# Two more LN2 tiles of the first block transposed by DMA, two more FFN blocks in halves, tile 3 loaded ahead of the keys' weight, and a new instruction order

## The chip, the cores and the metric

The kernel runs on one core of one Trainium2 chip. The metric is the device time of one launch in microseconds (us); a kernel's time is the median of several runs. Five engines work at once, each in the order of its own instruction list: TensorE (PE, matrix products and transposes), VectorE (DVE), ScalarE (ACT), GpSimd (POOL) and SyncE (SP), which here issues all the DMAs. They wait for each other through semaphores only where data or a buffer demands it.

## The reference

A linear-attention block and a feed-forward block, both with a layer norm ahead of them and a residual around them, on 2048 tokens of width 512, with 32 heads of 16 and a hidden width of 1792, in bf16:

```python
phi = lambda t: jnp.where(t > 0, t + 1, jnp.exp(t)) + 1e-6
pq, pk = phi(q), phi(k)
kv  = jnp.einsum("bhsd,bhse->bhde", pk, v)
z   = jnp.einsum("bhsd->bhd", pk)
num = jnp.einsum("bhqd,bhde->bhqe", pq, kv)
den = jnp.einsum("bhqd,bhd->bhq", pq, z)[..., None] + 1e-6
...
h  = x + _A_ref(_layernorm(x, axis=-1), A_wqkv, A_wo)   # q, k, v = layernorm(x) @ wqkv; (num / den) @ wo
h2 = h + _B_ref(_layernorm(h, axis=-1), B_w1, B_w2)     # relu(layernorm(h) @ w1) @ w2
```

## The kernel before

The order of all work is written out by hand in the string `ORDER`: 564 words, each of which emits one small group of instructions. `lx.3.1` loads one token tile from tile 3 on, `K.0.4` makes the keys of tile 0 in PSUM bank 4, and so on. The words are emitted in sequence, and each engine gets its own in that sequence; a word's place matters against the other words of its engine, and for waits against what it reads. Nothing is scheduled by a compiler.

The 2048 tokens are 16 tiles of 128 (`NT`), and 4 chunks of 512 (`NCH`), tiles 4c to 4c+3 being chunk c. PSUM has 8 banks of 128x512 f32; the bank is written into the words of PE (last number or second number), so a product waits until the bank's last contents have been read.

**Loads and first layer norm.** SP issues the loads of x (`lx`, line 214), then those of the weights (`lk` keys, `lq` queries, later `lv`, `lo`, `l1`, `l2`, line 220). For each tile t: `S.t`, `A.t` (DVE, mean and variance, lines 248, 249), `R.t.n` (ACT, two small instructions for the reciprocal deviation, lines 254, 255), `N.t` (DVE, line 262). The result must be transposed into `lnT[c]`: tiles 0 to 4 by PE (`T.t.bank`, four 128x128 transposes, line 287) with a copy by ACT (`E.t`, line 297), tiles 5 to 15 by a DMA transpose issued by SP (`X.t`, line 308). The words `warm` ahead of all this are products on zeros with no reader.

**Keys, queries, statistics.** `K.t` (line 316) and `Q.c.j` (line 324) are four products of 512 columns each. phi is made as `F`/`qF` (ACT, exp), `U`/`qU` (ACT, relu), `M`/`qM` (DVE), `D`/`qD` (DVE, line 344). `G.t` (line 368) adds tile t's layer norm times pk into banks 4 to 7, over all 16 tiles. The column sum z is gathered from DVE sums of tiles 2 to 9 (`za`, `zf`, `zhi`, `zlo`) and from the other tiles by forty products of one column (`z`, line 392), whose last operands are pk of tiles 14 and 15, written by `D.14.2`. Then come `zc`, `zh` on DVE, and `gA`/`gD`, `kv`, `kx`, `m`, `mA`/`mD`, which make the folded matrix `m_sb`.

**Denominators.** For chunk c: `d4` (PE, line 440; one word may do two chunks), `dl4` and `dx4` (ACT, lines 446, 451), `wb.c` (SP writes the reciprocals to DRAM, line 468), eight words `rb.c.h` (SP reads them back broadcast over heads into `rr`, line 471), `dm.c` (DVE, two instructions, line 484: queries times `rr` into `pqs`). `rr` is one buffer for all four chunks.

**Attention output and second layer norm.** `h.t` (PE, four products, line 493), `hD.t` (DVE, adds x), `s.t`, `a.t` (DVE, statistics), `r` (ACT, reciprocal deviations of four tiles), `n.t` (DVE, line 270) or `nA.t` (ACT, line 276) for the centred, negated tile in `hn`. It is transposed into `lnT[c]` either by SP with a DMA transpose (`x.t`, line 309) or by PE with a DVE copy (`t.t.bank`, line 287, and `v.t`, line 306). In the first chunk tiles 0 and 1 go by DMA, 2 and 3 by PE. All later tiles go by DMA.

**FFN.** `p.c.f` (PE, line 508) makes block f of 14 of the hidden layer for the 512 tokens of chunk c, four products of 512 columns. `ph.c.f.bank.half` (line 517) does the same for 256 tokens, four products of 256 columns, so that half 0 needs only tiles 0 and 1 of the chunk. Chunk 0 has blocks 0 to 3 in halves and the other ten whole. `pD` (DVE) or `pA` (ACT) empties two banks into `acts`. `f.t` (PE, line 537), `fo.t` (DVE, line 545) and `fd.t` (SP) make and store the output of tile t; the columns of the last tile are done in three parts.

Of the kernel before, what the change touches and what calls it, by code (L numbers as in the profile page):

```python
# [57 lines left out]
def kernel(  # L58
# [166 lines left out]
    def op_tw(n):
        rows = A_wqkv.rearrange("(r s) n -> r s n", s=A_wqkv.shape[0] // n)
        nc.scalar.dma_start(out=first_w[0:n, 0, :], in_=rows[:, 0, D : D + 4])

    def op_tx(n):
        rows = xf.rearrange("(r s) d -> r s d", s=S // n)  # L230
        nc.scalar.dma_start(out=first_x[0:n, :], in_=rows[:, 0, 0:4])

    def op_ta():
        nc.scalar.dma_start(out=first_w[:], in_=wqkv_v[:, :, D : D + 4])
# [234 lines left out]

    def op_rb(c, h):  # L470
        nc.sync.dma_start(
            out=rr[h * DH : (h + 1) * DH, :, :],
            in_=scr[c][:, h, :, :].rearrange("j o n -> o j n").broadcast_to([DH, KD, CW]),
        )
# [6 lines left out]

    def op_dm(c, jb, n):
        i = (c * KD + jb) % NQ
        nc.vector.tensor_tensor(  # L484
            out=pqs[:, i : i + n, :], in0=pqT[c][:, jb : jb + n, :], in1=rr[:, jb : jb + n, :], op=ALU.mult
        )


# [99 lines left out]
```

## Time and profile before

| what | value |
|---|---|
| median of three runs (lowest, highest) | 169.46 us (169.15, 169.84) |
| the profiled execution: its time | 169.66 us |
| the profiled execution: its span, first to last instruction | 168.0 us |
| granted TensorE clock, mean | 1.00 |
| DVE busy, ACT busy | 115.6 us, 49.5 us |

The span is what the trace shows; the profiled execution's time is 1.66 us longer than its span, for what lies around it. All durations come from this one execution. In the trace a product's own duration includes the filling and draining of its pipeline; products that follow each other overlap, so what a product costs PE is read from the chain of waits or from the distance of start times. "Idle before" is the time an engine stood still ahead of an instruction, with what ended it. In the rows, `x4` counts the instructions that a row merges.

### The profile page before, as it was taken

How to read it: one execution, taken by the hardware profiler on the slowest of the kernel's cores; microseconds unless marked ns; L12 is line 12 of the kernel's file. 1: busy time of each engine (PE TensorE's matmuls, PEld its weight loads, DVE VectorE, ACT ScalarE, POOL GpSimd, SP SyncE). 2: the span in 40 equal slices, each digit the busy share in tenths (PEclk: the TensorE clock that was granted, in tenths of full speed). 3: DMA queues.
4: the chain of work that ended last, by engine and by line, in shares of the span. 5: the costliest groups of instructions: out<-in, count | busy, mean ns of one | idle time of the engine just before them, and what ended most of it. 6: DMA issues, size and time to landing. Idle time of an engine off the chain costs nothing.

```text
span 168.0 us, 2417 instructions
## 1 busy us (share of the span) xinstructions
PE 162.7 (97%) x924; PEld 79.2 (47%) x924; DVE 115.6 (69%) x217; ACT 49.5 (29%) x83; POOL 4.8 (3%) x21
## 2 busy tenths in 40 slices
PE   7799999999999999999999999999999999999992
PEld 7444444454544754444444444444444447444442
DVE  3899999942579999999999755764144773432312
ACT  3799968715798843100101000000000000000000
POOL 7400000000000000000000000000000000000000
PEclk9999999999999999999999999999999999999999
DMA  4984054681595364414552520000101000011021
GB/s 108 353 298 88 20 106 95 189 301 45 132 337 161 98 205 132 132 48 123 83 102 57 126 63 0 0 0 0 62 31 35 0 0 7 32 34 48 31 94 39
DMA packets 25003, 16.01 MB, mean 95 GB/s; under 512 B 15008, under 2 KB 23968, under 8 KB 24992
## 3 DMA queue, kind: packets, MB, share of 16 engines
...
q8 instruction: 7, 0.11, 0.3%
...
## 4 chain that ended last, share of the span: by engine, by line
PE 92%; DMA 4%; SPq 2%; DVE 1%; issue 0%
PE bk L537 28%; PE bk L508 27%; PE bk L324 8%; PE bk L368 8%; PE bk L493 8%; PE bk L316 7%; DMA wq_sb<-in_A_wqkv_dram 4%; PE bk L517 2%; SPq L214 2%; PE bk L440 1%; DVE gT L545 1%; PE bk L392 1%; PE bk L414 1%; PE bk L426 1%; PE bk L287 0%
## 5 line engine op out<-in xcount | busy, mean ns | idle before, releaser
L537 PE MATMUL bk<-w_sb,at 128*128 128x512 bf16 (+2 forms) x252 | 50.0, 355 | 0.0
L508 PE MATMUL bk<-lnT,w_sb 128*128 128x512 bf16 x208 | 46.9, 379 | 0.0
L528 DVE TENSOR_SCALAR at<-bk 128x1024 bf16<-128x1024 f32 x27 | 32.8, 1223 | 13.2 <-PE bk L508 13.2
L537 PEld LDWEIGHTS <-at 128*128 128x128 bf16 x252 | 23.5, 98 | 25.4
L508 PEld LDWEIGHTS <-w_sb 128*128 128x128 bf16 x208 | 20.4, 98 | 23.9
L545 DVE SCALAR_TENSOR_TENSOR gT<-bk,rstd,h_nat 128x512 bf16<-128x512 f32 (+2 forms) x18 | 12.4, 691 | 24.6 <-PE bk L537 22.0
L334 ACT ACTIVATE eb<-bk 128x1024 bf16<-128x1024 f32 (+1 forms) x18 | 16.6, 929 | 5.3 <-PE bk L316 2.8
L337 ACT ACTIVATE rb<-bk 128x1024 bf16<-128x1024 f32 (+1 forms) x18 | 16.4, 929 | 0.0
L324 PE MATMUL bk<-lnT,wq_sb 128*128 128x512 bf16 x64 | 15.1, 379 | 0.3 <-DMA wq_sb<-in_A_wqkv_dram 0.3
L316 PE MATMUL bk<-wk_sb,lnT 128*128 128x512 bf16 x64 | 15.3, 379 | 0.0
L493 PE MATMUL bk<-m_sb,pqs 128*128 128x512 bf16 x64 | 15.1, 379 | 0.0
L368 PE MATMUL bk<-at,h_nat 128*128 128x512 bf16 x56 | 13.1, 379 | 0.0
L248 DVE BATCH_NORM_STATS2 st<-x_nat 128x6 f32<-128x512 bf16 x16 | 10.6, 678 | 2.3 <-DMA x_nat<-in_A_x_dram 2.3
L499 DVE TENSOR_TENSOR h_nat<-bk,x_nat 128x512 bf16<-128x512 f32 x16 | 10.6, 676 | 0.9 <-PE bk L493 0.9
L254 ACT ACTIVATE rstd<-mv,eps 128x2 f32<-128x2 f32 (+2 forms) x14 | 4.2, 297 | 23.7 <-DVE mv L251 20.9
L250 DVE BATCH_NORM_STATS2 st<-h_nat 128x6 f32<-128x512 bf16 x16 | 10.5, 684 | 0.1
L324 PEld LDWEIGHTS <-wq_sb 128*128 128x128 bf16 x64 | 6.1, 98 | 7.7 <-DMA wq_sb<-in_A_wqkv_dram 0.8
L493 PEld LDWEIGHTS <-pqs 128*128 128x128 bf16 x64 | 6.1, 98 | 7.7 <-DVE pqs L484 0.6
L368 PEld LDWEIGHTS <-h_nat 128*128 128x128 bf16 x64 | 6.1, 98 | 7.3 <-issue 0.2
L316 PEld LDWEIGHTS <-lnT 128*128 128x128 bf16 x64 | 6.1, 98 | 6.8
L341 DVE TENSOR_SCALAR eb<-eb 128x1024 bf16<-128x1024 bf16 (+1 forms) x18 | 6.6, 389 | 0.0
L262 DVE TENSOR_SCALAR h_nat<-x_nat,mv,rstd 128x512 bf16<-128x512 bf16 x16 | 6.3, 408 | 0.2 <-ACT rstd L255 0.2
...
## 6 DMA issues: line engine op xcount, KB each, us to landing
...
x_nat<-in_A_x_dram SPq DMA_DIRECT2D x2, 512.0 KB, 7.9
...
wk_sb<-in_A_wqkv_dram SPq DMA_DIRECT2D x1, 512.0 KB, 4.1
...
wq_sb<-in_A_wqkv_dram SPq DMA_DIRECT2D x1, 512.0 KB, 6.2
```

The costliest lines, as they stand in the source:

```text
L248: op_S = lambda t: nc.vector.bn_stats(out=st[:, t, :], in_=x_nat[:, t, :])
L316: nc.tensor.matmul(bk[:, b, :], lhsT=lnT[c][:, kd, j * P : (j + 1) * P], rhs=wk_sb[:, kd, :], start=(kd == 0), stop=(kd == KD - 1),)
L324: nc.tensor.matmul(bk[:, b, :], lhsT=wq_sb[:, kd, j * P : (j + 1) * P], rhs=lnT[c][:, kd, :], start=(kd == 0), stop=(kd == KD - 1),)
L334: nc.scalar.activation(out=buf(eb, kind, i, n), in_=bank(at_bank[kind, i], n), func=ACT.Exp)
L337: nc.scalar.activation(out=buf(rb, kind, i, n), in_=bank(at_bank[kind, i], n), func=ACT.Relu)
L368: nc.tensor.matmul(bk[:, KD + kd, :], lhsT=ln_nat[:, t, kd * P : (kd + 1) * P], rhs=pk(t)[:, 0, :], start=(not stated), stop=(len(stated) ...
L493: nc.tensor.matmul(bk[:, b, :], lhsT=pqs[:, (c * KD + jb) % NQ, j * P : (j + 1) * P], rhs=m_sb[:, jb, :], start=(jb == 0), stop=(jb == KD ...
L499: nc.vector.tensor_tensor(out=h_nat[:, t : t + n, :], in0=bank(at_bank["h", t], n), in1=x_nat[:, t : t + n, :], op=ALU.add,)
L508: nc.tensor.matmul(bk[:, b, :], lhsT=w1_sb[:, kd, f * P : (f + 1) * P], rhs=lnT[c][:, kd, :], start=(kd == 0), stop=(kd == KD - 1),)
L528: nc.vector.tensor_scalar(out=acts[c % 2][:, f : f + n, :], in0=bank(at_bank["p", c, f], n), scalar1=-1.0, scalar2=0.0, op0=ALU.mult, op1= ...
L537: nc.tensor.matmul(bk[:, b, 0 : w * P], lhsT=acts[c % 2][:, f, j * P : (j + 1) * P], rhs=w2_sb[:, f, k * P : (k + w) * P], start=(f == 0), ...
L545: nc.vector.scalar_tensor_tensor(out=o_t[:, t % NO, cols], in0=bk[:, at_bank["f", t, k], 0 : w * P], scalar=rstd2[:, t : t + 1], in1=h_nat ...
```

## The change

1. `lx.3.1` (load of tile 3) is issued before `lk.0.4` (the keys' weight) instead of after it.
2. `t.2`, `t.3` and their DVE copies `v.2`, `v.3` are gone; `x.2`, `x.3` (DMA transposes on SP) take their place. SP's list there becomes `wb.1 x.3 x.1 x.0 x.2 rb.1...` instead of `wb.1 x.1 x.0 rb.1...`. ACT makes the centred tile 3 (`nA.3`), DVE those of tiles 0, 1, 2; before, ACT made 0 and 1 and DVE 2 and 3.
3. FFN blocks 6 and 7 of chunk 0 are made in halves too: `ph` occurs 12 times instead of 8, `p` 50 times instead of 52.
4. `rr` becomes two buffers, used by chunk parity (`rr[c % 2]`). Four helpers that no word calls, and the two tiles they wrote, are deleted.
5. The whole `ORDER` is new. On PE, all four `T` of the first tiles stand ahead of `K.1`, and half of `K.3` ahead of the first `Q`; between `K.12` and `z` there are other `G`s, with eleven tiles' `G` ahead of `z` in place of twelve; `h.3`, `h.1` follow two of chunk 2's `Q`s in place of four; the first eight words after `Q.3` are halves.

PE's list around the loads, the sums and the second layer norm, before and after:

```
before: T.0 T.1 K.0 T.2 K.1 T.3 K.2 Q.0.3 T.4 Q.0.1 K.3 Q.0.0 K.4 ...
after:  T.0 T.1 K.0 T.2 T.3 K.1 K.2 K.3(first half) Q.0.0 K.3(second half) T.4 Q.0.1 Q.0.3 K.4 ...

before: ... K.12 G.7 K.11 K.10 G.8 K.14 K.15 G.9 G.6 G.10 G.11 z G.14 d4.0 G.13 G.12 G.15 Q.1.1 ...
after:  ... K.12 G.5 K.11 K.10 K.14 K.15 G.8 G.4 G.9 G.6 G.7 G.10 z G.14 d4.0 G.15 G.11 G.12 G.13 Q.1.1 ...

before: Q.2.0 Q.2.1 Q.2.3 Q.2.2 h.1 d4.1 h.0 h.2 h.3 Q.3.0 Q.3.1 Q.3.3 Q.3.2 t.2 t.3
        ph.3.0 ph.1.0 ph.2.0 ph.3.1 ph.0.0 ph.0.1 ph.2.1 p.7 d4.2 ph.1.1 p.6 h.4 ...
after:  Q.2.1 Q.2.0 h.3 h.1 d4.1 h.0 Q.2.2 Q.2.3 h.2 Q.3.2 Q.3.3 Q.3.0 Q.3.1
        ph.2.0 ph.3.0 ph.6.0 ph.7.0 ph.6.1 ph.7.1 ph.1.0 d4.2 ph.3.1 ph.2.1 ph.0.1 ph.0.0 ph.1.1 p.4 p.5 h.7 ...
        (ph.f.half, chunk 0)
```

The diff, with the two strings cut to the places that the prediction speaks of:

```diff
-table const masks warm.70.7.64 warm.2.7 lx.0.1 S.0 A.0 R.0.1 lx.1.1 S.1 lx.2.1 A.1 N.0 T.0.1 lk.0.4 S.2 R.1.1
-N.1 T.1.2 lx.3.1 A.2 E.0 K.0.4 R.2.1 lx.4.2 S.3 N.2 T.2.1 E.1 A.3 S.5 R.3.1 K.1.0.0.2 K.1.0.2.2 N.3 S.4 A.5 A.4
-E.2 T.3.2 K.2.6.0.2 K.2.6.2.2 F.0.1 M.0.1 lx.6.2 E.3 S.7 lq.0.4 R.4.2 lx.8.4 Q.0.3.1 N.4 U.0.1 A.7 F.1.1 F.2.1
...
-qD.1.2.2 mA.2.2 qF.2.0.2 Q.2.2.0 qU.2.0.2 dm.0.2.2 dm.0.0.2 qM.2.0.2 h.1.6 hD.1 s.1 a.1 qU.2.2.2 d4.1.3 dl4.1
-h.0.7 hD.0 s.0 dx4.1 h.2.6 h.3.5 a.0 l2.0.7 wb.1 hD.2 nA.1 hD.3 qF.2.2.2 nA.0 s.2 s.3 Q.3.0.2 Q.3.1.3 a.2
-Q.3.3.6 a.3 qF.3.0.2 qU.3.0.2 Q.3.2.5 x.1 r.0.4 qF.3.2.2 n.2 t.2.7 n.3 t.3.4 qD.2.0.2 v.2 v.3 x.0 ph.0.3.1.0
-ph.0.1.3.0 ph.0.2.0.0 ph.0.3.1.1 qM.2.2.2 qM.3.0.2 ph.0.0.2.0 ph.0.0.2.1 qM.3.2.2 qD.3.0.2 qU.3.2.2 qD.2.2.2
...
+table const masks warm.70.7.64 warm.2.7 lx.0.1 S.0 A.0 R.0.1 lx.1.1 S.1 A.1 lx.2.1 N.0 lx.3.1 R.1.1 S.2 N.1 A.2
+S.3 T.0.4 A.3 E.0 R.2.1 lk.0.4 N.2 R.3.1 N.3 T.1.0 K.0.1 T.2.7 lx.4.2 E.1 F.0.1 S.4 S.5 E.2 M.0.1 T.3.5
+K.1.0.0.2 E.3 A.5 A.4 K.1.0.2.2 lx.6.2 K.2.6.0.2 F.1.1 lq.0.4 R.4.2 S.7 S.6 lx.8.4 U.0.1 U.1.1 N.5 K.2.6.2.2 A.6
...
+m.1.3 m.3.7 qU.1.2.2 m.2.6 rb.0.1 rb.0.6 mD.0.2 qF.1.2.2 mA.2.2 Q.2.1.5 Q.2.0.4 rb.0.7 rb.0.5 dm.0.0.2 dm.0.2.2
+h.3.2 qM.1.2.2 qF.2.0.2 h.1.0 qD.1.2.2 l1.2.2 hD.3 l2.0.7 qU.2.0.2 hD.1 d4.1.3 s.3 a.3 s.1 h.0.6 Q.2.2.0 Q.2.3.1
+dl4.1 dx4.1 wb.1 nA.3 h.2.7 hD.0 a.1 n.1 x.3 qF.2.2.2 s.0 Q.3.2.3 Q.3.3.4 a.0 n.0 hD.2 s.2 x.1 x.0 a.2 n.2
+Q.3.0.6 Q.3.1.7 qM.2.0.2 qU.2.2.2 ph.0.2.0.0 ph.0.3.1.0 x.2 rb.1.7 qM.2.2.2 qF.3.2.2 qD.2.0.2 qM.3.2.2 r.0.4
+qU.3.2.2 rb.1.6 rb.1.2 rb.1.4 rb.1.1 ph.0.6.4.0 qD.2.2.2 qF.3.0.2 qD.3.2.2 qM.3.0.2 qU.3.0.2 qD.3.0.2 ph.0.7.5.0
+ph.0.6.4.1 ph.0.7.5.1 rb.1.3 rb.1.0 ph.0.1.3.0 d4.2.6.2 ph.0.3.1.1 ph.0.2.0.1 rb.1.5 dl4.2 pD.0.6.2 l2.7.7
+ph.0.0.2.1 ph.0.0.2.0 pD.0.2.2 dl4.3 ph.0.1.3.1 dm.1.0.2 p.0.4.4 p.0.5.5 dm.1.2.2 h.7.1 pD.0.0.2 h.5.6 h.4.3
...
-    rr = big.tile([P, KD, CW], BF16, name="rr")
+    rr = [big.tile([P, KD, CW], BF16, name=f"rr{i}") for i in range(2)]
...
     def op_rb(c, h):
         nc.sync.dma_start(
-            out=rr[h * DH : (h + 1) * DH, :, :],
+            out=rr[c % 2][h * DH : (h + 1) * DH, :, :],
...
     def op_dm(c, jb, n):
         i = (c * KD + jb) % NQ
         nc.vector.tensor_tensor(
-            out=pqs[:, i : i + n, :], in0=pqT[c][:, jb : jb + n, :], in1=rr[:, jb : jb + n, :], op=ALU.mult
+            out=pqs[:, i : i + n, :], in0=pqT[c][:, jb : jb + n, :], in1=rr[c % 2][:, jb : jb + n, :], op=ALU.mult
         )
```

More of the change, by code (lines that the diff above doesn't have):

```diff
@@ L29 @@
-lo.0.2 lo.2.2 zc zh d4.0.1 dl4.0 l1.0.2 G.13 G.12 G.15 dx4.0 gA.2.2 Q.1.1.3 Q.1.0.2 qF.1.0.2 gD.0.2 kv.1.4
-kv.3.4 kv.0.4 kv.2.4 kx qU.1.0.2 qM.1.0.2 qD.1.0.2 Q.1.3.1 Q.1.2.0 qF.1.2.2 m.0.2 m.1.3 mD.0.2 m.3.7 m.2.6 wb.0
-Q.2.0.4 Q.2.1.5 rb.0.7 rb.0.1 rb.0.6 rb.0.3 rb.0.0 rb.0.2 rb.0.4 rb.0.5 l1.2.2 qM.1.2.2 qU.1.2.2 Q.2.3.1
-qD.1.2.2 mA.2.2 qF.2.0.2 Q.2.2.0 qU.2.0.2 dm.0.2.2 dm.0.0.2 qM.2.0.2 h.1.6 hD.1 s.1 a.1 qU.2.2.2 d4.1.3 dl4.1
-h.0.7 hD.0 s.0 dx4.1 h.2.6 h.3.5 a.0 l2.0.7 wb.1 hD.2 nA.1 hD.3 qF.2.2.2 nA.0 s.2 s.3 Q.3.0.2 Q.3.1.3 a.2
@@ new lines @@
+S.3 T.0.4 A.3 E.0 R.2.1 lk.0.4 N.2 R.3.1 N.3 T.1.0 K.0.1 T.2.7 lx.4.2 E.1 F.0.1 S.4 S.5 E.2 M.0.1 T.3.5
+K.1.0.0.2 E.3 A.5 A.4 K.1.0.2.2 lx.6.2 K.2.6.0.2 F.1.1 lq.0.4 R.4.2 S.7 S.6 lx.8.4 U.0.1 U.1.1 N.5 K.2.6.2.2 A.6
+A.7 lx.12.4 K.3.7.0.2 R.6.2 Q.0.0.2 K.3.7.2.2 N.4 M.1.1 S.9 N.6 A.9 D.1.1 D.0.1 T.4.0 Q.0.1.3 F.2.1 U.2.1 S.8
+E.4 Q.0.3.1 N.7 F.3.1 A.8 qF.0.0.2 R.8.2 S.11 K.4.5 X.5 M.2.1 M.3.1 qU.0.0.2 K.5.6 F.4.2 U.4.2 A.11 S.12 N.9
+A.12 N.8 S.13 U.3.1 Q.0.2.0 D.2.1 A.13 S.10 S.15 X.6 R.12.2 N.13 A.10 X.7 X.9 K.6.2 K.7.3 A.15 U.6.2 qM.0.0.2
@@ new lines @@
+D.3.1 N.12 G.2 G.1 G.0 S.14 R.10.2 N.11 G.3 A.14 F.6.2 X.8 X.13 N.10 M.6.2 M.4.2 qF.0.2.2 qU.0.2.2 qD.0.0.2
+K.9.3 X.12 D.4.2 R.14.2 N.14 N.15 qM.0.2.2 D.6.2 K.8.2 F.8.2 U.8.2 M.8.2 K.13.1 K.12.0 qD.0.2.2 X.11 za.4.1 G.5
+F.12.2 K.11.3 M.12.2 D.8.2 X.10 za.6.0 K.10.2 U.12.2 F.10.2 M.10.2 U.10.2 X.14 K.14.0 za.8.0 X.15 D.12.2 K.15.1
+zf lv.2.2 D.10.2 zhi U.14.2 G.8 G.4 F.14.2 M.14.2 lv.0.2 zlo lo.0.2 D.14.2 G.9 G.6 G.7 G.10 z.3.1 z.2.1 z.1.1
+z.0.1 zc zh G.14 d4.0.2 dl4.0 dx4.0 lo.2.2 G.15 G.11 G.12 G.13 Q.1.1.3 gA.0.2 l1.0.2 gD.2.2 wb.0 Q.1.0.2 rb.0.3
@@ new lines @@
+qU.3.2.2 rb.1.6 rb.1.2 rb.1.4 rb.1.1 ph.0.6.4.0 qD.2.2.2 qF.3.0.2 qD.3.2.2 qM.3.0.2 qU.3.0.2 qD.3.0.2 ph.0.7.5.0
+ph.0.6.4.1 ph.0.7.5.1 rb.1.3 rb.1.0 ph.0.1.3.0 d4.2.6.2 ph.0.3.1.1 ph.0.2.0.1 rb.1.5 dl4.2 pD.0.6.2 l2.7.7
+ph.0.0.2.1 ph.0.0.2.0 pD.0.2.2 dl4.3 ph.0.1.3.1 dm.1.0.2 p.0.4.4 p.0.5.5 dm.1.2.2 h.7.1 pD.0.0.2 h.5.6 h.4.3
+hD.7 s.7 hD.5 a.7 hD.4 h.6.1 p.0.12.0 hD.6 dx4.2 wb.2 rb.2.4 rb.2.7 s.4 s.6 dx4.3 s.5 p.0.9.6 p.0.11.3 rb.2.3
+a.4 a.6 a.5 pA.0.4.2 rb.2.2 rb.2.1 rb.2.0 rb.2.5 n.7 n.6 n.4 rb.2.6 n.5 dm.2.2.2 p.0.8.5 dm.2.0.2 wb.3 rb.3.4
@@ new lines @@
+f.0.7.0.7 p.0.13.1 rb.3.0 pD.0.8.2 h.8.4 p.0.10.2 pD.0.12.2 hD.8 pD.0.10.2 x.6 h.11.5 h.9.0 rb.3.5 rb.3.1 rb.3.3
+rb.3.2 rb.3.6 s.8 hD.9 h.10.6 a.8 hD.11 hD.10 rb.3.7 s.9 x.7 s.11 s.10 a.9 a.11 a.10 n.9 f.3.2.0.7 f.3.2.7.7
+f.2.4.0.7 dm.3.0.2 dm.3.2.2 n.10 n.8 n.11 f.2.4.7.7 fo.3 h.15.0 h.14.3 hD.15 s.15 hD.14 h.12.2 r.4.4 a.15 hD.12
+h.13.0 x.5 s.14 hD.13 s.12 x.4 x.11 p.1.1.1 f.0.7.7.7 p.1.6.2 r.8.4 p.1.0.0 a.14 s.13 a.12 a.13 n.15 n.14 n.13
+n.12 fo.2 fo.0 x.10 x.9 p.1.8.6 p.1.7.3 f.1.5.0.7 fd.2 pD.1.0.2 f.1.5.7.7 pD.1.6.2 fo.1 p.1.9.7 p.1.12.2
@@ new lines @@
+p.1.13.3 fd.3 pD.1.8.2 pD.1.12.2 p.1.2.5 p.1.3.6 p.1.5.2 p.1.4.1 x.8 pD.1.2.2 p.1.11.7 p.1.10.6 x.14 pD.1.4.2
+pD.1.10.2 p.2.6.2 p.2.7.3 p.2.11.7 p.2.10.6 pD.2.6.2 p.2.4.4 x.15 fd.0 fd.1 pD.2.10.2 p.2.5.5 pD.2.4.2 p.2.0.2
+p.2.1.3 pD.2.0.2 f.7.4.0.7 f.7.4.7.7 fo.7 f.4.6.0.7 fd.7 x.12 f.4.6.7.7 fo.4 f.6.5.0.7 f.6.5.7.7 x.13 fd.4 fo.6
+f.5.6.0.7 f.5.6.7.7 fo.5 p.3.6.1 p.3.7.2 pD.3.6.2 p.3.5.5 p.3.4.4 pD.3.4.2 p.3.10.2 p.3.11.3 r.12.4 pD.3.10.2
+p.3.1.6 p.3.0.5 pD.3.0.2 p.3.3.3 p.3.2.2 pD.3.2.2 p.3.9.7 p.3.8.6 pD.3.8.2 p.3.12.1 p.3.13.2 p.2.12.3 pD.3.12.2
@@ L54 @@
+f.15.7.0.14.2.1 f.15.2.0.14.0.2 p.2.13.4 p.2.3.6 p.2.2.5 fo.15.2.1 fo.15.0.2 pD.2.12.2 p.2.9.4 p.2.8.3 pD.2.2.2
+pD.2.8.2 f.14.1.0.7 f.14.1.7.7 f.9.7.0.7 f.9.7.7.7 f.13.6.0.7 fd.5 fd.6 fo.14 fo.9 fd.9 fd.15.2.1 fd.15.0.2
+f.13.6.7.7 fo.13 fd.13 fd.14 f.12.0.0.7 f.12.0.7.7 fo.12 f.11.6.0.7 f.11.6.7.7 f.10.7.0.7 fo.11 fd.11 f.10.7.7.7
+f.8.0.0.7 fo.10 fd.12 fd.10 f.8.0.7.7 fo.8 fd.8 f.15.1.0.14.3.1 fo.15.3.1 fd.15.3.1
 """
@@ L108 @@
     w2_v = B_w2.rearrange("(k p) n -> p k n", p=P)
-    first_w = const.tile([P, KD, 4], BF16, name="first_w")
-    first_x = const.tile([P, 4], BF16, name="first_x")
     x_nat = big.tile([P, NT, D], BF16, name="x_nat")
@@ L223, in op_ak @@
         nc.scalar.dma_start(out=wk_sb[:, k : k + n, :], in_=wqkv_v[:, k : k + n, D : 2 * D])
[L225 to L234, printed above, removed]
     op_lk = lambda k, n: load_d(wk_sb, wqkv_v[:, :, D : 2 * D], k, n)
@@ L478, in op_rs @@
         nc.sync.dma_start(
-            out=rr[:, j, :], in_=rows.rearrange("h (o n) -> h o n", o=1).broadcast_to([P // DH, DH, CW])
+            out=rr[c % 2][:, j, :], in_=rows.rearrange("h (o n) -> h o n", o=1).broadcast_to([P // DH, DH, CW])
         )
```

26 lines of the change are left out of this document (1 added, 25 removed).

## The prediction

> **What bounds the kernel now.** I read the page's busy times first, then the busy times by stretch of the span, then the chain of waits, and only then the rows around the places that the change touches.
>
> ```profile
> span 168.0 us, 2417 instructions
> PE 162.7 (97%) x924; PEld 79.2 (47%) x924; DVE 115.6 (69%) x217; ACT 49.5 (29%) x83; POOL 4.8 (3%) x21
> ...
> 0.00:10.38 10.38, 8.06 (x101) 5.43 (x101) 7.10 (x24) 6.42 (x17) 4.80 (x21) 1.00 0.81 263
> 10.38:35.65 25.27, 25.27 (x121) 11.59 (x122) 24.49 (x60) 20.76 (x34) 0.00 (x0) 1.00 0.51 125
> 35.65:164.20 128.55, 128.55 (x695) 61.56 (x694) 82.92 (x132) 22.33 (x33) 0.00 (x0) 1.00 0.27 77
> 164.20:168.00 3.80, 0.77 (x14) 0.59 (x11) 1.10 (x2) 0.00 (x0) 0.00 (x0) 1.00 0.14 43
> ```
>
> The columns by stretch are its length, then the busy time of PE, PE's weight loads, DVE, ACT and POOL, the granted clock, the DMA share and GB/s. Between 10.38 and 164.20 PE is never idle (25.27 of 25.27, 128.55 of 128.55 us) and its clock is full. So PE's list is the time: work taken from it after 10.38 comes off the end, work done before 10.38 comes off too, and each moment in which PE has to wait is added. Only in the second stretch is another engine near its limit: DVE, 24.49 of 25.27.
>
> ```profile
> 4.16 6.17 DMA wq_sb<-in_A_wqkv_dram
> 10.38 1.04 PE bk L324 x4
> ...
> 12.50 0.86 PE bk L316 x4
> ...
> 35.81 0.98 PE bk L392 x40
> ...
> 56.70 0.45 PE bk L287 x8
> 57.15 3.06 PE bk L517 x28
> ...
> 61.07 0.55 PE bk L440 x8
> ...
> 101.01 12.09 PE bk L508 x56
> ...
> 165.00 0.35 DVE gT L545
> ```
>
> The chain of waits, in order of time (start, us, what): SP's loads up to the queries' weight, landing at 10.33, then PE to the end, a copy and a store. From it come PE's prices: four products of 512 columns 0.86, eight transposes 0.45 (four 0.22), a d4 of two chunks 0.55.
>
> **The change part by part.** Removed, t.2 and t.3: 0.45 us of PE (row 56.70), sum −0.45. Their two copies leave DVE, which is not the bound there.
>
> Added, two blocks in halves: a product of 256 columns costs 3.06/28 = 0.109, one of 512 12.09/56 = 0.216, so a block costs 8 × 0.109 instead of 4 × 0.216, +0.01; for two +0.02.
>
> The start. The rows of the timeline (start, us, engine, line, what; in brackets the idle time before and its end):
>
> ```profile
> 2.66 1.45 SPq L214 DMA_DIRECT2D x_nat<-in_A_x_dram  x3
> 5.95 0.16 DVE L249 BATCH_NORM_AGGREGATE mv<-st 128x2 f32<-128x6 f32 x1
> 6.62 0.69 DVE L248 BATCH_NORM_STATS2 st<-x_nat 128x6 f32<-128x512 bf16 x1 [0.51 <-DMA x_nat<-in_A_x_dram]
> 7.23 0.40 DVE L262 TENSOR_SCALAR h_nat<-x_nat,mv,rstd 128x512 bf16<-128x512 bf16 x1
> ...
> 7.75 0.29 ACT L254 ACTIVATE rstd<-mv,eps 128x1 f32<-128x1 f32 x1 [0.59 <-DVE mv L249]
> 8.19 0.58 ACT L297 ACTIVATE lnT<-bk 128x512 bf16<-128x512 bf16 x1
> 8.66 0.59 ACT L334 ACTIVATE eb<-bk 128x512 bf16<-128x512 f32 x1
> ...
> wk_sb<-in_A_wqkv_dram SPq DMA_DIRECT2D x1, 512.0 KB, 4.1
> ```
>
> S.3 stood 0.51 us for tile 3, issued at 2.66; issued one place (0.48) earlier, it lets S.3 begin behind A.2, at about 6.05. Then A.3 ends at 6.95, R.3 (0.44 on ACT, 7.75 to 8.19) at 7.45, N.3 (0.40) at 7.9, T.3 (0.22) at 8.2. ACT takes an instruction of this size every 0.47 (8.19 to 8.66): E.1 from 7.45, F.0 7.92, E.2 8.39, E.3 8.86 to 9.44. PE: K.1 8.2, K.2 9.06 to 9.93, half of K.3 (0.43) to about 10.4. So PE meets the first Q at 10.40 instead of 10.38, with 0.43 more behind it: −0.41. The keys' weight is issued 0.48 later and took 4.1; landing at 6.8 at the latest by that, K.0 (0.86) and T.2 (0.22) are done by 7.9, when T.3 can start, so it costs nothing unless it is later still. Bounds: −0.43 if all fits, +0.1 if that weight lands a full us later and the queries' weight slips with it.
>
> The sum z:
>
> ```profile
> 34.39 0.69 DVE L344 TENSOR_TENSOR at<-rb,eb 128x1024 bf16<-128x1024 bf16 x1
> ...
> 35.65 0.19 PE L392 MATMUL bk<-ones,zhl 128*128 128x1 bf16 x2
> ```
>
> The last operand (D.14) was ready at 35.08, and PE came at 35.65, 0.57 later. In the new order one G (0.86) less stands ahead of z, and PE is 0.41 early: it comes at 34.38, and reads D.14 a quarter us later, at 34.6. DVE has the same instructions to do until then, and is nearly full: D.14 can only come earlier by idle time that goes. The 0.51 ahead of S.3 goes; N.3 now waits some 0.2 to 0.3 for R.3. D.14 would end at 34.7 to 34.9, so PE waits +0.1 to +0.3; I take +0.1, since the DMA transposes and ACT's work ahead of it also come earlier (two to three Gs, moved behind K.14 and K.15). Bounds 0, and +0.5 if DVE gains nothing.
>
> The turn from m to h:
>
> ```profile
> 45.51 1.23 DVE L432 CAST m_sb<-bk 128x1024 bf16<-128x1024 f32 x1 [0.34 <-PE bk L426]
> 46.91 1.03 ACT L429 ACTIVATE m_sb<-bk 128x1024 bf16<-128x1024 f32 x1
> 47.78 1.29 DVE L484 TENSOR_TENSOR pqs<-pqT,rr 128x1024 bf16<-128x1024 bf16 x2
> 49.20 1.03 PE L493 MATMUL bk<-m_sb,pqs 128*128 128x512 bf16 x4
> ```
>
> From here on I give times in the clock of before; the shift so far is the same for all engines. h.3 comes two Qs (1.73) sooner than h.1 did, at 47.47. dm.0 now follows mD directly: two instructions from 46.7 to 47.95; mA ends at 47.94. The third of h.3's four products, due at 47.90, needs both: +0.1. If `rr`, which was in time for a dm at 47.78, is later than 46.7, it is more: d4.0 has moved forward by one G, 0.86, so at worst 0.2 more. Bounds 0, as PE cannot come to h.3 sooner than its list allows, and +0.3.
>
> The second layer norm of tiles 0 to 3, where SP's list grows:
>
> ```profile
> 50.61 0.69 ACT L446 ACTIVATE ld<-bk,eps 128x512 f32<-128x512 f32 x1
> 51.33 0.63 ACT L451 ACTIVATE rd<-ld 128x512 bf16<-128x512 f32 x1
> 51.93 0.72 ACT L276 ACTIVATE hn<-h_nat,mv 128x512 bf16<-128x512 bf16 x1
> ...
> 54.20 1.20 SPq L309 DMA_TRANSPOSE lnT<-hn  x1
> lnT<-hn SPq DMA_TRANSPOSE x1, 2.4
> ...
> 22.01 2.53 SPq L308 DMA_TRANSPOSE lnT<-h_nat  x2
> ...
> 56.54 0.61 PE L287 MATMUL bk<-ident,hn 128*128 128x128 bf16 x8
> ...
> 55.58 3.73 SPq L471 DMA_DIRECT2D rr<-scr  x8
> ...
> 61.92 1.29 DVE L484 TENSOR_TENSOR pqs<-pqT,rr 128x1024 bf16<-128x1024 bf16 x2 [0.20 <-DMA rr<-scr]
> ```
>
> Before, x.0 was issued at 54.20 and landed 2.4 later, at 56.6, under the transposes on PE; the first half-block began at 56.99. Now the half-block is due when Q.3 ends, 56.54 + 0.1 = 56.64. Two transposes go ahead of x.0: d4.1 has two Qs less and one h more ahead of it and comes 0.86 earlier, so dl4.1 starts at 49.75, dx4.1 at 50.47, nA.3 at 51.1, done at 51.85, and x.3 leaves at 51.9. Each takes SP about 1.27 (two in 2.53): x.1 53.2, x.0 54.45, landing 56.9. PE waits +0.25. That is where 0.45 of removed transposes is partly paid back. Bounds: 0, if the chain is 0.25 faster; the upper one is the rival below. x.2 lands 1.27 after x.0, at 58.15; the fifth half-block is due at 56.9 + 4 × 0.44 = 58.65, so the two added blocks cover it; without them (three halves) 58.2 would be no cover.
>
> Behind them wait the eight rb.1: they start at 57.0, 1.4 later than 55.58, so that dm.1 can start at 61.92 + 1.4 = 63.35 and has both halves at 64.65. h.7 is due at 56.9 + 12 × 0.44 + 0.55 (d4.2) + 1.73 = 64.45, its third product at 64.9: nothing, with 0.2 to spare. The second `rr` buffer frees rb.3 from waiting for dm.2; PE was not waiting there, so nothing. The end has the same last words (14 products of 128 columns, a copy of 0.35, a store): nothing.
>
> **Sum:** −0.45 + 0.02 − 0.41 + 0.1 + 0.1 + 0.25 = −0.39. The profiled execution took 169.66 (span 168.0 and 1.66 around it), so 169.27; it lies 0.20 above the median of 169.46, and the median becomes 169.07, say 169.1. Own range 168.7 to 169.6.
>
> **The rivals.** *All of it arrives.* No wait at z, h.3 and x.0: −0.45 + 0.02 − 0.43 = −0.86, 168.6. For it: the waits I find are 0.1 to 0.25 long and each rests on differences of that size. Against: three places must all be better than I read them. This is also the floor, as PE has nothing else to lose.
>
> *DVE takes over at z.* D.14 ends at 35.08 as before, PE waits 0.5 instead of 0.1: −0.39 + 0.4 = 0.0, 169.5. For it: 24.49 of 25.27 busy; any new wait on DVE is handed on one for one. Against: the 0.51 of idle time that goes.
>
> *The transposes on SP are slow (slower than before).* One of the same kind behaved otherwise:
>
> ```profile
> 11.10 1.83 SPq L308 DMA_TRANSPOSE lnT<-h_nat  x1
> lnT<-h_nat SPq DMA_TRANSPOSE x1, 3.4
> ```
>
> It was issued while loads were in flight, took SP 1.83 and landed after 3.4. If x.3, x.1, x.0 meet the loads of the FFN's weights in the same way, x.0 lands at 51.9 + 2 × 1.83 + 3.4 = 58.95, PE waits 2.3 instead of 0.25, and rb.1 and h.7 slip with it: −0.39 + 2.05 = +1.65, 171.1. It is slower than before from the point where x.0 lands 0.4 later than I have it, and by over 0.5% from 1.25 later. Against: x.1 and x.0 took 1.2 and 2.4 there before. A rule speaks for this rival: the Trainium skill, "VectorE: DVE Perf Modes", section "Rules for kernel authors", would have a 128x128 transpose on TensorE wherever PSUM will do as its target, and its section on the three paths gives the crossbar DMA 1309 ns against 390. By these figures, as an estimate, a tile's four transposes would cost TensorE 1.56 us and the change would be worth far more than I reckon, so the figures plead for the change and the rule against it; the trace has 0.22 for the four back to back, and 2.4 for the DMA, and agrees with the rule as far as delay goes.
>
> **How the numbers follow.** Forecast 0.37, all of it 0.2, DVE at z 0.18, slow transposes 0.25. A measurement of this kernel tells about 0.5% from no change, 0.85 us: below 168.6 and above 170.3. The floor is just at 168.6, so faster holds half of that rival and a little of the forecast's low end: 0.2. Slower holds most of the slow transposes and a rest for several small waits that add up: 0.28. Within: 0.52. The range runs from 0.2 under the floor to near the last rival, 168.4 to 170.9.
>
> **What would show it.** Right: the first Q at about 10.4 with half of K.3 before it; S.3 with no wait; idle PE of about 0.1 ahead of z and of h.3, 0.25 ahead of the first half-block, put down to DVE and to the DMA into `lnT`; none ahead of h.7. Wrong: PE idle over 0.3 anywhere between 10.4 and the end, the queries' weight landing after 10.8, or a transpose that takes SP over 1.5 us.

## The result, and the profile after

| kernel | median (lowest, highest), runs | profiled execution: time, span |
|---|---|---|
| before | 169.65 us (169.15, 170.39), 4 | 169.66, 168.0 |
| after | 171.59 us (171.09, 172.31), 4 | 171.37, 169.6 |

The changed kernel takes 1.0112 times as long as before, with an interval of 1.0085 to 1.0139: about 1.9 us slower, where 0.4 us faster was forecast. It lies outside the range of 168.4 to 170.9.

The page of the changed kernel, and its busy times by stretch with the same bounds as before:

```profile
span 169.6 us, 2394 instructions
PE 161.9 (95%) x908; PEld 79.9 (47%) x924; DVE 115.7 (68%) x216; ACT 48.6 (29%) x82; POOL 4.8 (3%) x21
...
10.38:35.65 25.27, 25.09 (x154) 12.02 (x157) 24.12 (x61) 20.11 (x33) 0.00 (x0) 1.00 0.60 156
35.65:164.20 128.55, 125.81 (x636) 60.20 (x647) 83.08 (x130) 21.82 (x32) 0.00 (x0) 1.00 0.26 73
```

The clock is still full. In the third stretch PE, which was never idle there before, now lacks 2.74 us. The timeline puts 2.16 of them down to two waits, in the brackets below. The rest are small pieces where the record of a product is missing (908 products for 924 weight loads). The rows of PE, DVE and SP on which the account rests:

```profile
10.34 1.03 PE L311 MATMUL bk<-lnT,wq_sb 128*128 128x512 bf16 x4
13.59 1.89 PE L303 MATMUL bk<-wk_sb,lnT 128*128 128x512 bf16 x7
...
33.65 0.69 DVE L331 TENSOR_TENSOR at<-rb,eb 128x1024 bf16<-128x1024 bf16 x1
34.31 0.19 PE L379 MATMUL bk<-ones,zhl 128*128 128x1 bf16 x2
...
56.80 3.22 PE L504 MATMUL bk<-lnT,w_sb 128*128 128x256 bf16 x28 [0.47 <-issue]
64.42 3.62 PE L480 MATMUL bk<-m_sb,pqs 128*128 128x512 bf16 x16
...
73.97 1.29 DVE L471 TENSOR_TENSOR pqs<-pqT,rr 128x1024 bf16<-128x1024 bf16 x2 [2.18 <-DMA rr<-scr]
75.32 0.55 PEld L480 LDWEIGHTS <-pqs 128*128 128x128 bf16 x4 [1.96 <-DVE pqs L471]
75.55 0.81 PE L480 MATMUL bk<-m_sb,pqs 128*128 128x512 bf16 x3 [1.69 <-DVE pqs L471]
...
51.36 1.52 SPq L296 DMA_TRANSPOSE lnT<-hn  x1
52.97 1.22 SPq L296 DMA_TRANSPOSE lnT<-hn  x1
54.28 2.53 SPq L296 DMA_TRANSPOSE lnT<-hn  x2
56.90 3.35 SPq L458 DMA_DIRECT2D rr<-scr  x7
60.77 0.43 SPq L218 DMA_DIRECT2D w_sb<-in_B_w_dram  x1
62.21 0.34 SPq L455 DMA_DIRECT2D scr<-rd  x1
66.77 4.88 SPq L458 DMA_DIRECT2D rr<-scr  x8
```

The big wait is the 1.69 ahead of `h.8`, the first product that reads chunk 2's `dm`. Here, too, a record is missing: `h.8` has four weight loads, from 75.32, but only three products, from 75.55. A product takes 0.22, so the first one started at about 75.33 and PE really stood still for 1.47. DVE stood 2.18 us for `rr` before it could start `dm.2`, at 73.97 (before: 71.47). On SP the eight `rb.2` start at 66.77, although their reciprocals were sent to DRAM by `wb.2` at 62.21. What stands between them and before is a load: `l2.7.7`, the second half of the FFN's second weight, 896 KB, issued at 60.77. The same place before the change:

```profile
59.35 0.43 SPq L220 DMA_DIRECT2D w_sb<-in_B_w_dram  x1
63.27 0.34 SPq L468 DMA_DIRECT2D scr<-rd  x1
65.17 3.89 SPq L471 DMA_DIRECT2D rr<-scr  x8
...
71.47 1.29 DVE L484 TENSOR_TENSOR pqs<-pqT,rr 128x1024 bf16<-128x1024 bf16 x2
```

Before, 3.9 us lay between the load and `wb.2`, and `rb.2` could start 1.9 after `wb.2`. Now it is 1.4, because the load comes 1.42 later (SP is busy longer with transposes and `rb.1`) and `wb.2` 1.06 earlier (its `d4.2` stands earlier in PE's list), and `rb.2` starts 4.56 after `wb.2`. A second delay comes on top: the eight `rb.2` now take SP 4.88 instead of 3.89, 0.99 more. So `dm.2` is 2.50 later than before because `rb.2` starts 1.60 later and then goes out more slowly. The chain of waits of the changed kernel runs through this place; before, it ran on PE alone from 10.38 to the last copies:

```profile
47.16 1.83 PE bk L480 x8
...
56.33 0.47 issue
56.80 3.22 PE bk L504 x28
...
62.21 4.54 DMA scr<-rd
...
66.77 0.32 SPq L458
...
76.36 0.86 PE bk L495 x4
...
165.69 0.76 DVE gT L532
```

Rows of the same view before, for the account:

```profile
73.38 2.59 PE bk L493 x12
75.97 1.51 PE bk L537 x7
...
164.22 0.77 DVE gT L545
```

**The account**, on the chain's clock. The start gained 0.47 (`K.4` at 13.59 instead of 14.06, with the same work ahead of it). The first two `h` took 1.83 for eight products instead of 1.73: +0.10, so `Q.3` ends at 56.33, 0.37 earlier than before (56.70). The transposes taken off PE gave −0.45, the halves +0.02. The first half-block cost 0.63: 0.47 idle, and its 28 products stand in the chain with 3.22 instead of 3.06. The timeline has 3.22 for them in both kernels (56.99 before, 56.80 after): in a running stream a product starts 0.16 before the one ahead of it has ended, and behind a stop this overlap is missing. At `h.8`: before, the first `h` of chunk 2 ended at 73.38 + 0.86 = 74.24; the new order has one block less (0.86) and one group of seven output products more (1.51) ahead of that point, so 74.89 with nothing else changed; it ended at 76.36, +1.47 in all. Without `h.8`'s own wait the sum to there is −0.47 + 0.10 − 0.45 + 0.02 + 0.63 = −0.17, so that wait cost 1.64. It can be read directly too: 1.47 idle and 0.16 of overlap are 1.63. From there to the last copies nothing is gained or lost: 165.69 against 164.22 is +1.47 again. The two profiled executions differ by 1.71; of the remaining 0.24, 0.13 lies between the last copy and the end of the span and 0.11 outside it, and neither was traced.

### The profile page after: what moved, and what is told of

Same layout as the page of the kernel before. It is cut to its first block, busy times and chain, and to the rows that moved or that the text cites. A ratio compares the mean times of both kernels' runs of the same rounds, so it can differ in the third digit from the quotient of the medians.

```text
span 169.6 us, 2394 instructions
## 1 busy us (share of the span) xinstructions
PE 161.9 (95%) x908; PEld 79.9 (47%) x924; DVE 115.7 (68%) x216; ACT 48.6 (29%) x82; POOL 4.8 (3%) x21
## 4 chain that ended last, share of the span: by engine, by line
PE 83%; DMA 4%; DVE 4%; issue 3%; SPq 2%; ACT 1%; DVEq 0%
PE bk L524 27%; PE bk L495 22%; PE bk L355 8%; PE bk L311 8%; PE bk L303 7%; PE bk L480 6%; DMA scr<-rd 3%; SPq L458 2%; PE bk L504 2%; DVE st L235 2%; DMA x_nat<-in_A_x_dram 1%; ACT ld L433 1%; DVE gT L532 1%; PE bk L427 1%; PE bk L379 1%
## 5 line engine op out<-in xcount | busy, mean ns | idle before, releaser
L524 PE MATMUL bk<-w_sb,at 128*128 128x512 bf16 (+2 forms) x248 | 49.4, 355 | 0.2
L495 PE MATMUL bk<-lnT,w_sb 128*128 128x512 bf16 x196 | 44.3, 379 | 0.2
L495 PEld LDWEIGHTS <-w_sb 128*128 128x128 bf16 x200 | 19.6, 98 | 23.2
L303 PE MATMUL bk<-wk_sb,lnT 128*128 128x512 bf16 x62 | 14.7, 379 | 0.2
L471 DVE TENSOR_TENSOR pqs<-pqT,rr 128x1024 bf16<-128x1024 bf16 x8 | 5.2, 688 | 2.5 <-DMA rr<-scr 2.5
```

Source lines behind the costliest of these rows:

```text
L303: nc.tensor.matmul(bk[:, b, :], lhsT=lnT[c][:, kd, j * P : (j + 1) * P], rhs=wk_sb[:, kd, :], start=(kd == 0), stop=(kd == KD - 1),)
L495: nc.tensor.matmul(bk[:, b, :], lhsT=w1_sb[:, kd, f * P : (f + 1) * P], rhs=lnT[c][:, kd, :], start=(kd == 0), stop=(kd == KD - 1),)
L524: nc.tensor.matmul(bk[:, b, 0 : w * P], lhsT=acts[c % 2][:, f, j * P : (j + 1) * P], rhs=w2_sb[:, f, k * P : (k + w) * P], start=(f == 0), ...
```

## The experiments

Times of the kernel before in the three sets of runs: 169.69 (29 runs), 169.68 (23), 169.62 (18). Ratios are against these, with their intervals. The changed kernel was not run again in these sets; where an experiment is compared with it, its 171.59 is meant.

**Is it the load ahead of `wb.2`?** The theory: the write waits for the load, so moving the load behind `rb.2` gives the 1.69 back and leaves the rest. In the rival, `rb.2` are late for another reason (SP's longer list, slow broadcasts), and moving the load would give back little.

`e1_w2_behind_rb2`, the changed kernel with one word moved in `ORDER` (only SP's words shown):

```diff
 rb.1.5
-l2.7.7
 wb.2
...
 rb.2.6
+l2.7.7
 wb.3
```

> The changed kernel with one DMA moved: the second half of w2 (l2.7.7, 896 KB) is issued behind the eight rb.2 instead of ahead of wb.2. Theory, collision: wb.2 (issued 62.2) landed only 0.3 us behind that load, after 4.5 us; without the load ahead of it it lands in about 1.9, rb.2 starts at 64.1 instead of 66.8, dm.2 waits for nothing, the 1.69 us of idle PE ahead of h.8 are gone: about 169.9. The load itself is not needed before the second half of f.3 at 81. Rival, the longer SP list (two more transposes): everything behind them on SP is late by 1.3 us whatever the load does, so h.8 keeps at least 1 us of its wait: 171 or more.

Measured: 170.22 us, ratio 1.0031 (1.0004 to 1.0058), 1.4 us below the changed kernel; the rival had said 171 or more. SP and PE in this run:

```profile
62.74 0.34 SPq L456 DMA_DIRECT2D scr<-rd  x1
64.49 3.92 SPq L459 DMA_DIRECT2D rr<-scr  x8
68.46 0.43 SPq L219 DMA_DIRECT2D w_sb<-in_B_w_dram  x1
68.99 0.49 SPq L456 DMA_DIRECT2D scr<-rd  x1
74.11 0.78 SPq L459 DMA_DIRECT2D rr<-scr  x2
...
57.33 3.22 PE L505 MATMUL bk<-lnT,w_sb 128*128 128x256 bf16 x28 [0.73 <-ACT rb L325]
74.23 1.03 PE L481 MATMUL bk<-m_sb,pqs 128*128 128x512 bf16 x4
```

`rb.2` starts 1.75 after `wb.2`, and the wait ahead of `h.8` is gone. The load now stands right ahead of `wb.3`, whose readers start 5.12 after it; that costs nothing here, as no wait on PE follows. What is left over the kernel before is the wait at the first half-block, 0.73 in this execution.

The opposite, `e2_before_w2_later`: the kernel before, with three small loads (four columns of x each, into a buffer that is free then) put ahead of that load, so that SP comes to it later (only SP's words shown).

```diff
+    def op_pad(n, i):
+        rows = xf.rearrange("(r s) d -> r s d", s=S // n)
+        nc.sync.dma_start(out=first_w[0:n, i, :], in_=rows[:, 0, 0:4])
...
 rb.1.5
+pad.128.0 pad.128.1 pad.128.2
 l2.7.7
 wb.2
```

> The kernel before with three tiny loads (4 columns of x each, read by nobody) on SP ahead of l2.7.7, so that this load is issued some 1.35 us later (about 60.7 instead of 59.35), as in the changed kernel; nothing else is changed. Collision: wb.2 (63.3) lands at about 66.6 instead of 65.17, rb.2 and dm.2 slip by 1.4, and PE stands still ahead of h.10 for 0.5 to 1.3 us: 170.2 to 171.0. If the load does not matter for the write, no change: 169.6.

Measured: 171.53 us, ratio 1.0117 (1.0074 to 1.016): the kernel before becomes as slow as the changed one. The load is issued at 61.31 instead of 59.35, `rb.2` starts at 66.82 instead of 65.17, and a wait stands ahead of chunk 2's `h`, which came at 73.22 before:

```profile
61.31 0.44 SPq L221 DMA_DIRECT2D w_sb<-in_B_w_dram  x1
...
66.82 3.90 SPq L476 DMA_DIRECT2D rr<-scr  x8
...
74.27 2.93 PE L498 MATMUL bk<-m_sb,pqs 128*128 128x512 bf16 x12 [0.37 <-DVE pqs L489]
```

It was 0.5 to 1.3 more than expected: the load came 1.96 later, where 1.35 had been reckoned with. And not all of the loss is the collision. This execution is late ahead of it too: 0.13 at the first `Q` (10.51), 0.36 by the second `d4` (50.52 instead of 50.16) and 0.52 behind `h.4` (64.24 instead of 63.72), whose `dm.1` began 0.53 later. From there to chunk 2's last `h` (78.64 instead of 77.32) 0.80 more is lost; that is the price of the late write here. At the last copies it is 1.35 in all (165.57 against 164.22). So e2 shows the wait where the theory puts it, but its median should not be read as the price.

**Does the kernel before have the same slack to give?** `e11_before_w2_behind_rb2` makes e1's move in the kernel before (`l2.7.7` from ahead of `wb.2` to behind `rb.2.7`).

> The kernel before with l2.7.7 behind rb.2: a control. There wb.2 landed 0.3 us behind that load too, but after 1.9 us and with no wait of dm.2; the load's place is worth nothing there: 169.7. If the write gains over 0.5 us and the time falls, the kernel before was paying for this as well.

Measured: 171.17 us, ratio 1.0096 (1.007 to 1.0122). The expectation was wrong.

```profile
69.75 0.49 SPq L469 DMA_DIRECT2D scr<-rd  x1
76.09 0.78 SPq L472 DMA_DIRECT2D rr<-scr  x2
...
83.55 1.29 DVE L485 TENSOR_TENSOR pqs<-pqT,rr 128x1024 bf16<-128x1024 bf16 x2 [3.06 <-DMA rr<-scr]
```

It is the same collision one write further: the load is issued at 69.23, 0.52 ahead of `wb.3`, `rb.3` can start only 6.34 after that write, and `dm.3`, which began at 80.65 before, waits 3.06; PE then stands 1.84 ahead of the `h` of chunk 3. e1 escaped this for two reasons: in the new order the `h` of chunk 3 come later (84.59 in e1, 82.72 in the kernel before), and the load landed about 2.0 sooner than here (table). It is a third kernel in which the same two DMAs in the same neighbourhood make the same wait, this time for another chunk.

Seven executions side by side; the load's landing is its issue plus the time from issue to landing that the profile gives to a tenth:

| kernel | load issued | load landed | write issued | its readers start |
|---|---|---|---|---|
| before | 59.35 | 64.85 | 63.27 (`wb.2`) | 65.17 |
| e3 (below) | 58.73 | 64.2 | 62.37 (`wb.2`) | 64.52 |
| e2 | 61.31 | 66.4 | 63.63 (`wb.2`) | 66.82 |
| e9_w2_ahead_of_wb2 (below) | 60.78 | 66.1 | 62.51 (`wb.2`) | 66.44 |
| after | 60.77 | 66.4 | 62.21 (`wb.2`) | 66.77 |
| e1 | 68.46 | 73.7 | 68.99 (`wb.3`) | 74.11 |
| e11 | 69.23 | 75.7 | 69.75 (`wb.3`) | 76.09 |

The readers start 0.3 to 0.5 after the load has landed, wherever in the 5 to 6.5 us of the load the write was issued; in the other seven kernels run it is 0.3 to 0.6. With no load ahead of it, `wb.2` takes 1.75 until they start (e1; 1.72 to 1.76 in the five other kernels with the load behind `rb.2`). So in the kernel before the two just met: 63.27 + 1.75 = 65.02, 0.15 before the 65.17 at which its readers started. A load is not the only thing that a write can be late behind: `wb.3`, issued behind the eight `rb.2` with no load in flight, landed after 4.0 in the kernel before and 3.3 in e5, but after 2.2 in the changed kernel. What held it was not looked into; PE did not wait for it.

**The two added transposes.** `e3_tiles23_by_pe`: the changed kernel with tiles 2 and 3 transposed on PE again.

```diff
-x.3
...
 Q.3.1.7
+t.3.5 t.2.2
...
-x.2
...
+v.3 v.2
 qD.2.0.2
```

> The changed kernel with part 2 undone: tiles 2 and 3 of the first chunk are transposed by PE (t.3, t.2 behind Q.3, copies by DVE), SP has only x.1 and x.0; all else as changed. Collision by way of SP: rb.1 and l2.7.7 are issued some 2.5 us earlier, l2.7.7 is 4 us ahead of wb.2 as in the kernel before, wb.2 lands in 2 us, no wait ahead of h.8 (-1.69) and none ahead of the first half-block (-0.47), at a price of 0.45 for the transposes: about 169.9. If the new order is at fault and not the transposes: 171 to 172.

Measured: 170.39 us, ratio 1.0032 (1.0013 to 1.0051). Both waits are gone, as SP is free 2 us sooner (the load at 58.73 instead of 60.77):

```profile
60.69 0.40 PE L428 MATMUL bk<-pqT,zhd 128*32 128x512 bf16 x4 [0.51 <-DVE pqT L332]
```

It missed the expected 169.9 by a new wait, 0.51 ahead of the second chunk of `d4.2`: DVE, which now has the copies `v.3` and `v.2` too, finishes chunk 3's queries later. `e5_pe_t_d4_later` moves that word back by a half-block's place:

```diff
-d4.2.6.2 ph.0.3.1.1 ph.0.2.0.1
+ph.0.3.1.1 ph.0.2.0.1 d4.2.6.2
```

> Tiles 2 and 3 transposed by PE as in e3, and d4.2 two half-blocks later in PE's list (behind ph.2.1). In e3 PE stood 0.51 us ahead of d4.2's second chunk, waiting for qD.3.0 on DVE; nothing else was lost. If that is all that e3 lacked, 170.4 - 0.5 = 169.9, and PE has no wait over 0.1 between 56 and 80. If wb.2, now 0.9 later, brings rb.2 too late for dm.2, the wait comes back ahead of h.8.

Measured: 169.91 us, ratio 1.0014 (0.9995 to 1.0034); no wait on PE after the first `Q`. So the loss came by way of SP's list: with the transposes back on PE, and that one word moved, 1.7 us of the 1.9 are gone, although PE pays its 0.45 again. e1, which leaves the transposes on SP, shows that they do this harm mainly by pushing the load towards `wb.2`.

**Keeping the transposes on SP, and taking both waits out.** `e4_both_waits_out` is e1 with SP's order x.1 x.0 x.3 x.2 (tiles 0 and 1 are needed first) and one more first half ahead of the second halves:

```diff
-x.3
...
-x.1 x.0
 a.2 n.2
+x.1 x.0 x.3 x.2
...
-x.2
...
+ph.0.1.3.0
 ph.0.6.4.1
...
-ph.0.1.3.0
 d4.2.6.2
```

> The changed kernel with l2.7.7 behind rb.2 as in the first run, and SP's four transposes as x.1 x.0 x.3 x.2, and the half-block ph.1.0 of the first two tiles moved ahead of the first halves that need tiles 2 and 3. If x.0 behind x.3 was the cause of the 0.47 us ahead of the first half-block, that wait goes too and the start's and the transposes' gain shows: 169.65 - 0.45 - 0.47 + 0.2 for small gaps = about 168.9. If the wait has another cause, 169.4; if x.2 now comes too late for the second halves, 0.3 of it returns there.

Measured: 170.04 us, ratio 1.0014 (0.9996 to 1.0031), 1.1 above the expectation.

```profile
52.20 5.14 SPq L297 DMA_TRANSPOSE lnT<-hn  x4
57.44 3.81 SPq L459 DMA_DIRECT2D rr<-scr  x8
...
56.12 3.54 PE L505 MATMUL bk<-lnT,w_sb 128*128 128x256 bf16 x28
63.49 1.29 DVE L472 TENSOR_TENSOR pqs<-pqT,rr 128x1024 bf16<-128x1024 bf16 x2 [1.04 <-DMA scr<-rd]
```

The first half-block starts at 56.12, with no wait: what had held it was x.0 standing behind x.3. But the four transposes keep SP until 57.34, so x.2 is late for the second halves (28 products in 3.54 instead of 3.22) and `rb.1` late for `h.7`: 0.54 later than in the changed kernel, `dm.1` waits 1.04. That is in the profiled execution, which was the fastest of the twelve (169.69); the 0.35 that the median has above it can't be read there. `e6_more_halves_first` puts a further first half ahead (`ph.0.0.2.0` in front of `ph.0.6.4.1`), which cures the first of the two:

> e4 with one more half-block of tiles 0 and 1 (ph.0.0) ahead of the first that needs tiles 2 and 3. In e4 x.2 landed at 58.5, and the second halves were due at 58.3; SP's list is the same, so rb.1 still starts at 57.4 and h.7 still waits some 0.35 us. SP as the limit: 0.2 to 0.4 better than e4 at most: 169.7 to 170.0. If SP's list were no limit, the whole 0.75 us that e4 lost between 56 and 65 would go: 169.3.

Measured: 170.13 us, ratio 1.0021 (1.0004 to 1.0037): no better than e4. The second halves have no wait, but PE still comes to `h.7` too early:

```profile
64.22 3.80 PE L481 MATMUL bk<-m_sb,pqs 128*128 128x512 bf16 x16 [0.24 <-DVE pqs L472]
```

SP has not the time for four transposes and eight broadcasts there. `e6_rb1_from_gpsimd` is the same kernel with the eight `rb.1` issued by GpSimd:

```diff
     def op_rb(c, h):
-        nc.sync.dma_start(
+        (nc.gpsimd if c == 1 else nc.sync).dma_start(
```

> The same, with the eight rb.1 issued by GpSimd's queue (idle after 5 us) instead of SP, so that they do not stand behind the four transposes but start when wb.1 has landed, at about 53. If SP's order is what makes h.7 wait, dm.1 no longer waits and h.7 is in time: 0.35 better than the run beside it, about 169.4. If issuing from GpSimd is slow or disturbs the transposes in flight, no gain or a loss of a us or more.

Measured: 172.74 us, ratio 1.0192 (1.0149 to 1.0235), the second of its two expectations.

```profile
53.99 4.64 POOL L459 DMA_DIRECT2D rr<-scr  x8 [47.83 <-DMA scr<-rd]
lnT<-hn SPq DMA_TRANSPOSE x4, 4.6
...
58.73 2.78 PE L505 MATMUL bk<-lnT,w_sb 128*128 128x256 bf16 x24 [1.82 <-DMA lnT<-hn]
```

The broadcasts now run beside the transposes instead of behind them, and these land after 4.6 us in the median (2.4 to 4.9), so that PE waits 1.82 for the first half-block. Behind each other on one queue was better than side by side.

**One transpose fewer on SP.** `e9_one_tile_by_pe` takes only tile 3 back to PE, in the kernel of e6_more_halves_first: SP's list is x.1 x.0 x.2, and the load is behind `rb.2`.

```diff
-x.3
...
 Q.3.1.7
+t.3.2
...
 qD.2.0.2
+v.3
```

> Between e5 and the second e6 kind (more halves first): tile 3 goes by PE (t.3, 0.22 us), SP has x.1 x.0 x.2, and l2.7.7 is behind rb.2. SP's list as the limit: rb.1 starts 1.3 us earlier (56.2), x.2 lands at 57.7 ahead of the second halves at 58.5, h.7 waits for nothing; only 0.22 of the 0.45 is spent: better than e4 and e5 by 0.3 to 0.5, about 169.5, and, if the start's 0.3 to 0.4 shows, a little under the kernel before. Rival: transposes on SP are not the limit between 56 and 65: 170.0 as e4.

Measured: 169.50 us, ratio 1.0008 (0.9986 to 1.0031). SP is with `rb.1` at 56.92, and PE is never idle from 35.65 to the last copies at 163.93 (164.22 before), by the busy times of that stretch:

```profile
35.65:163.93 128.28, 128.28 (x666) 61.50 (x663) 83.38 (x133) 21.82 (x32) 0.00 (x0) 1.00 0.26 73
```

It has the lowest median of the new order's versions and is equal to the kernel before; the intervals of e4 and e5 overlap with its own. `e9_w2_ahead_of_wb2` puts only the load back to its place ahead of `wb.2` in it:

> The same with l2.7.7 back ahead of wb.2. Here it is issued at about 60.0, some 2 us ahead of wb.2 (62). Collision: it takes 5.5 us to land, and wb.2 lands 0.3 us behind it, at 65.8 instead of 63.9; rb.2 ends at 69.6 and lands at 72.2, and h.8 is due at 73.7: the write is late by 2 us in the trace and PE waits for 0 to 0.5 us of it: 169.5 to 170. So the price depends on the gap: 3.9 us free (before), 2 us nearly, 1.4 us 1.69.

Measured: 170.50 us, ratio 1.0061 (1.0035 to 1.0086), 1.0 above its twin and 0.5 above what was expected, as the gap was smaller than the 2 us reckoned with.

```profile
74.70 1.04 PE L481 MATMUL bk<-m_sb,pqs 128*128 128x512 bf16 x4 [0.97 <-DVE pqs L472]
```

Here the load goes out 1.73 ahead of `wb.2` (the table), and the wait of 0.97 ahead of `h.8` is the difference in time. This pair, equal but for the place of one load, isolates the price of the collision best. Part of it is again a slower `rb.2`: the eight take SP 4.66 here and 3.88 in the twin.

**The two parts thought cheap.** `e7_tile3_after_weight` undoes the first part in the changed kernel (the keys' weight ahead of tile 3's load):

```diff
-lx.3.1
...
 lk.0.4
+lx.3.1
```

> The changed kernel with the keys' weight loaded ahead of tile 3 again (part 1 undone, same order else). S.3 waits 0.5 us again, and with it R.3, N.3 and T.3, which now stand ahead of K.1: the first Q comes some 0.3 us later, at 10.65, and the median is 171.6 + 0.3 = 171.9. If the load order is covered, no change: 171.6.

Measured: 172.07 us, ratio 1.013 (1.0084 to 1.0176). The first `Q` is at 10.97 instead of 10.34; the medians differ by 0.48, but the intervals of the two ratios overlap. `e8_one_rr` undoes the two buffers:

```diff
-    rr = [big.tile([P, KD, CW], BF16, name=f"rr{i}") for i in range(2)]
+    rr = [big.tile([P, KD, CW], BF16, name="rr")] * 2
```

> The changed kernel with one rr buffer for all chunks (part 4 undone). rb.3 must wait for dm.2 again: it starts at 75.3 instead of 74.0, and dm.3 is not due until 83.9: no change, 171.6. If the second buffer shortens the wait ahead of h.8 by letting rb.1 or rb.2 go earlier, 172 or more.

Measured: 172.13 us, ratio 1.0141 (1.0119 to 1.0162). `rb.3` starts at 76.11 instead of 73.99, as it now waits for `dm.2`, and PE is not idle for it. The 0.5 us between the medians is within the two intervals, and the start alone was 0.29 later in the profiled execution; a price of the single buffer is not shown.

## Why the prediction was wrong

The step that failed is the paragraph on the eight `rb.1`: "Behind them wait the eight rb.1 … nothing, with 0.2 to spare." Its conclusion held: `rb.1` started at 56.90, 0.21 later than reckoned (57.0 in the clock of before, less the shift of 0.31), and `h.7` came with no wait at 64.42. But it followed SP's lengthened list only to its first reader. Next in that list stand `l2.7.7` and `wb.2`. Both rows were in the trace of before, and the sum had no term for them. Four facts made the collision: SP 1.42 later at the load, PE 1.06 earlier at `wb.2`, a write that ends only behind the load, and a `dm.2` that PE waits for. The move of `d4.2` in PE's list is in the change's text and was costed for `h.7` alone.

| step | predicted | measured |
|---|---|---|
| start | −0.41 | −0.47, half of `K.3` ahead of or behind the first `Q` as read |
| z behind D.14 | +0.1 | 0: D.14 ended at 34.34, PE began z at 34.31 |
| turn to h.3 | +0.1 | +0.10 |
| transposes off PE, halves | −0.43 | −0.43 |
| first half-block | +0.25 | +0.63 |
| h.7 behind rb.1 | 0 | 0 |
| h.8 behind `rb.2` | no term | +1.64 |
| sum | −0.39 | +1.47 |

The first half-block's term was right in kind and too small by 0.38. PE could have started it 0.16 earlier than reckoned, at 56.17 (the end of `Q.3` at 56.33, less the overlap of 0.16) instead of 56.64 less 0.31: the start gained 0.06 more, and the 0.10 at z did not come. And x.0 was later: x.3 took SP 1.52 instead of 1.27, x.0 left at 54.28, 0.14 later than reckoned, and PE began at 56.80, 2.52 after that, where 2.45 had been reckoned. In a chain of waits, the idle time alone (0.47) understates the cost of a stop by the overlap that is missing behind it.

The rival of slow transposes gave 171.1, near the time that came, by another mechanism: the longest transpose among them took 1.52 on SP and landed after 2.7, not 1.83 and 3.4 (no weight load was in flight: the last had landed at 50.8), and the price was paid some 19 us later, behind a load that no rival named. A right size is no proof of a mechanism; e1 tells the two apart, since it leaves the transposes as they are and gives 1.4 us back. On the rule of the Trainium skill that the prediction weighed against the change ("VectorE: DVE Perf Modes", "Rules for kernel authors"): it pointed the right way. e3, e5 and e9, with two or one of the tiles back on PE, are all faster than the changed kernel, e9 with the load and two half-blocks moved as well.

The start's gain varies. In the ten kernels run with tile 3's load ahead of the keys' weight, the first `Q` of the profiled execution came between 10.29 and 10.92, at 10.56 in the mean, against 10.48 in the three of the old order. With 0.43 of `K.3` done ahead of it the mean gain is some 0.35, an estimate from these few. K.0 waited up to 0.73 for the keys' weight:

```profile
7.11 1.02 PE L304 MATMUL bk<-wk_sb,lnT 128*128 128x512 bf16 x4 [0.71 <-DMA wk_sb<-in_A_wqkv_dram]
```

This is of e9_one_tile_by_pe, whose first `Q` came at 10.62. The prediction had this weight's landing at 6.8 at the latest, with a bound of +0.1; it landed later in this execution.
